# Decode attention over a 4096-key window: keys and values loaded as interleaved pairs of heads in 16 KB rows, the key work of each pair split by rows between VectorE and TensorE

## The chip, the cores and the metric

One core of one Trainium2 chip. The metric is the device time of one execution in microseconds (us). The kernel before took 196.72 us (median of 3 runs, 196.56 to 196.92).

## The reference, cut to what matters

```python
# x: 1 x 1 x 512; k_cache, v_cache: 1 x 32 heads x 32768 x 128, bf16; only the last W = 4096 keys count
q = (layernorm(x) @ wq)                        # 32 heads of 128
scores = q . k_cache[:, :, -4096:] * 128**-0.5 # one query per head
o = softmax(scores) @ v_cache[:, :, -4096:]
s = o.reshape(4096) @ wo                       # wo: 4096 x 512
return x + s * silu(block_B(layernorm(x)))     # B: a small MLP; its first mixing stage sees one position and gives zero
```

Keys and values are 32 heads x 1 MB each, 67.1 MB of the 78.8 MB that the program reads. There is one query per head, so every key and every value is used once.

## The kernel before

```python
G, LAG, K_BUFS, V_BUFS, MOVED = 4, 7, 12, 7, (2, 4)

def load_kv(pool, cache, h):                  # one head, 1 MB: 32 rows of 128 to a partition, 8 KB in one piece
    t = pool.tile([P, NC, Dh], BF16, tag="kv", name="kv")
    load(t[:], cache[0, h, W0:, :].rearrange("(p c) d -> p c d", p=P))
    return t

def k_vector(h, kn):                          # even heads: VectorE multiplies and sums
    ...
    nc.vector.tensor_tensor(out=prod[:], in0=kn[:], in1=q_bc[...].to_broadcast([P, NC, Dh]), op=ALU.mult)
    nc.vector.tensor_reduce(out=st[g]["sS"][:, hl // 2, :], in_=prod[:], axis=AX.X, op=ALU.add)

def k_turn(h, kn):                            # odd heads: TensorE transposes, ScalarE evacuates,
    for b in range(NB):                       # and TensorE multiplies with the query (k_scores)
        pt = ps_tr.tile([P, 8, P], BF16, tag="pt", name="pt")
        for i in range(8):
            nc.tensor.transpose(pt[:, i, :], kn[:, b * 8 + i, :], ident_bf[:])
        nc.scalar.copy(out=kts[h][:, b * 8:(b + 1) * 8, :], in_=pt[:])

for i in range(H + LAG):                      # value head h runs LAG behind key head i
    h = i - LAG
    kn = load_kv(k_pool, A_k_cache, i) if i < H else None
    ...
    v = load_kv(v_pool, A_v_cache, h) if h >= 0 else None
    ...
    if h == H - 1:                            # behind the last values: the output-weight rows of four heads,
        load_rows(H - G, G - 1)               # 512 KB in pieces of 1 KB
        load_rows(H - 1, 1)
    ...                                       # key work, then softmax of a group of four heads, then v_head
for h in range(H - G, H):
    y_head(h)                                 # four row products a head into y_ps
...
nc.vector.tensor_tensor(out=y[:], in0=y_ps[:], in1=g_row[:], op=ALU.mult)     # "the final product"
```

## Time and profile before

| | kernel before |
|---|---|
| time of the profiled execution, span in the profile | 197.07, 195.2 us |
| data moved by the main queue, packets | 78.85 MB, 11344 |
| PE, DVE, ACT busy | 134.2, 124.6, 85.0 us |
| last value head landed, final product began | 189.99, 191.73 us |

The prediction below shows the lines for the busy row, the queue, the chain and the tail. From the timeline of VectorE around the start (columns: start us, us, engine, line, operation, out<-in, count, idle time before and what ended it): the first product with a key.

```profile
25.46 2.29 DVE L278 TENSOR_TENSOR prod<-kv,q_bc 128x4096 bf16<-128x4096 bf16 x1 [1.32 <-ACT q_bc L242]
```

### The profile page before, as it was taken

What the parts mean: (1) busy time and instruction counts of PE and PEld (TensorE: products, weight loads), DVE (VectorE), ACT (ScalarE), POOL (GpSimd) and SP (SyncE); (2) the same over time, 40 slices, a digit from 0 to 9 for tenths busy, and PEclk for the clock granted to TensorE, in tenths of its full rate; (3) what the DMA queues carried; (4) which work ended last, traced back from release to release, by engine and by line L of the source; (5) the groups of instructions that cost most, each with busy time, mean ns of one, the idle gap of its engine ahead of it and who ended that gap; (6) DMA issues with size and microseconds to landing.
All of it is one profiled execution on the core that took longest, in us unless ns stands there. A gap on an engine that the chain in (4) does not pass through costs nothing.

```text
span 195.2 us, 4912 instructions
## 1 busy us (share of the span) xinstructions
PE 134.2 (69%) x2204; PEld 107.8 (55%) x2204; DVE 124.6 (64%) x124; ACT 85.0 (44%) x180; POOL 5.9 (3%) x13
## 2 busy tenths in 40 slices
PE   0559796814994987469988358289788477196952
PEld 0453456803993986464546357174547366195742
DVE  1520279998998988917877674909885678611101
ACT  2003066862954738343366318161638245173010
POOL 2110033000000000000000000000000000000000
PEclk9999998885555555557999855559999555555555
DMA  5999999999999999999999999999999999999980
GB/s 193 408 467 430 384 421 425 413 423 430 421 425 420 423 426 425 421 421 428 430 425 421 421 430 430 423 425 420 428 428 423 425 421 426 423 428 427 421 327 12
DMA packets 11516, 79.15 MB, mean 405 GB/s; under 512 B 1384, under 2 KB 2248, under 8 KB 2504
## 3 DMA queue, kind: packets, MB, share of 16 engines
q1 hardware_dynamic: 11344, 78.85, 96.6%
q8 instruction: 17, 0.28, 0.6%
q10 hardware_dynamic: 152, 0.00, 0.0%
q14 instruction: 3, 0.02, 0.0%
HBM read 78.84 MB, written 0.00 MB: 404 GB/s over the span
## 4 chain that ended last, share of the span: by engine, by line
DMA 81%; PE 12%; issue 3%; DVE 2%; ACT 1%; POOL 1%; SPq 1%; POOLq 0%
DMA kv<-in_A_k_cache_dram 51%; DMA kv<-in_A_v_cache_dram 28%; PE pt L290 2%; DMA x_bf<-in_A_x_dram 2%; PE qb_ps L240 2%; PE hr_ps L214 2%; PE a_ps L203 1%; PE hr_ps L211 1%; PE oT L389 1%; PE qT_ps L231 1%; SPq L77 1%; ACT kt L291 1%; DVE hr L217 0%; PE y_ps L141 0%; PE ln_ps L158 0%
## 5 line engine op out<-in xcount | busy, mean ns | idle before, releaser
L291 ACT COPY kt<-pt 128x1024 bf16<-128x1024 bf16 x64 | 60.1, 1025 | 48.5 <-PE pt L290 48.5
L281 DVE TENSOR_REDUCE sS<-prod 128x32 f32<-128x4096 bf16 x16 | 70.7, 4420 | 0.6
L290 PE MATMUL pt<-ident_bf,kv 128*128 128x128 bf16 x512 | 48.6, 277 | 18.6 <-DMA kv<-in_A_k_cache_dram 17.1
L290 PEld LDWEIGHTS <-kv 128*128 128x128 bf16 x512 | 44.3, 129 | 22.5 <-DMA kv<-in_A_k_cache_dram 19.6
L278 DVE TENSOR_TENSOR prod<-kv,q_bc 128x4096 bf16<-128x4096 bf16 x16 | 36.6, 2286 | 9.6 <-DMA kv<-in_A_k_cache_dram 8.2
L389 PE MATMUL oT<-pT,kv 128*128 128x1 bf16 x768 | 24.1, 165 | 9.4 <-DMA kv<-in_A_v_cache_dram 9.0
L389 PEld LDWEIGHTS <-kv 128*128 128x128 bf16 x768 | 22.9, 104 | 12.3 <-DMA kv<-in_A_v_cache_dram 9.7
L297 PE MATMUL sT<-qT_bf,kt 128*128 128x1 bf16 x512 | 16.4, 164 | 1.9 <-ACT kt L291 1.7
L297 PEld LDWEIGHTS <-kt 128*128 128x128 bf16 x512 | 15.1, 100 | 4.1 <-ACT kt L291 2.3
L379 PE MATMUL ov<-kv,pT 128*4 128x512 bf16 x64 | 15.7, 389 | 1.0 <-DMA kv<-in_A_v_cache_dram 1.0
L404 ACT ACTIVATE o<-oT,rden 128x1 bf16<-128x1 f32 x32 | 6.2, 263 | 16.3 <-PE oT L389 16.3
L336 DVE RECIPROCAL rden<-den_ps 128x4 f32<-128x4 f32 x8 | 1.5, 182 | 16.4 <-PE den_ps L334 16.4
L379 PEld LDWEIGHTS <-pT 128*4 128x4 bf16 x64 | 5.0, 85 | 8.6 <-issue 2.6
L311 PE MATMUL mt_ps<-ident_f,m 128*4 128x128 f32 x8 | 2.9, 359 | 9.1 <-DVE m L305 8.9
L321 PEld LDWEIGHTS mb_ps<-md,ones_f 4*128 4x128 f32 x16 | 3.6, 275 | 6.7 <-DVE md L315 6.5
L321 PE MATMUL mb_ps<-md,ones_f 4*128 4x4 f32 x16 | 4.3, 334 | 4.4 <-DVE md L315 4.4
L313 DVE TENSOR_REDUCE mx<-mt_ps 4x1 f32<-4x128 f32 x8 | 2.2, 278 | 7.7 <-PE mt_ps L311 7.7
L323 ACT COPY mb<-mb_ps 128x4 f32<-128x4 f32 x8 | 1.4, 173 | 12.8 <-PE mb_ps L321 12.8
L311 PEld LDWEIGHTS mt_ps<-ident_f,m 128*4 128x4 f32 x8 | 0.7, 94 | 10.1 <-issue 6.2
L551 DVE TENSOR_TENSOR y<-y_ps,g_row 128x128 f32<-128x128 f32 x1 | 0.3, 291 | 9.2 <-PE y_ps L141 9.2
L217 DVE COPY hr<-hr_ps 1x512 f32<-1x512 f32 x1 | 0.7, 679 | 8.1 <-PE hr_ps L214 8.1
L206 ACT ACTIVATE a_bf<-a_ps 128x10 bf16<-128x10 f32 x1 | 0.2, 180 | 11.5 <-PE a_ps L203 11.5
(110 smaller groups left out, 99.3 us busy)
## 6 DMA issues: line engine op xcount, KB each, us to landing
kv<-in_A_k_cache_dram SPq DMA_DIRECT2D x32, 1024.0 KB, 19.7
kv<-in_A_v_cache_dram SPq DMA_DIRECT2D x32, 1024.0 KB, 19.6
wq_sb<-in_A_wq_dram SPq DMA_DIRECT2D x1, 4096.0 KB, 18.1
wo<-in_A_wo_dram SPq DMA_DIRECT2D x3, 1024.0 KB, 19.6
w_sb<-in_B_w_dram SPq DMA_DIRECT2D x1, 1376.0 KB
w_sb<-in_B_w_dram SPq DMA_DIRECT2D x1, 1024.0 KB
w_sb<-in_B_w_dram SPq DMA_DIRECT2D x1, 512.0 KB, 3.8
wo_rows<-in_A_wo_dram SPq DMA_DIRECT2D x1, 384.0 KB, 15.5
```

The lines of the kernel that those rows point to most:

```text
L214: nc.tensor.matmul(hr_ps[:], lhsT=a_bf[0:m, i:i + 1], rhs=w4_sb[0:m, i, :], start=False, stop=(i == len(chunks) - 1))
L240: nc.tensor.matmul(qb_ps[:], lhsT=xn_rep[:, c, :], rhs=wq_h[:, c, 2 * i:2 * i + 8:2, :], start=(c == 0), stop=(c == KC - 1))
L278: nc.vector.tensor_tensor(out=prod[:], in0=kn[:], in1=q_bc[:, h // 2:h // 2 + 1, :].to_broadcast([P, NC, Dh]), op=ALU.mult)
L281: nc.vector.tensor_reduce(out=st[g]["sS"][:, hl // 2, :], in_=prod[:], axis=AX.X, op=ALU.add)
L290: nc.tensor.transpose(pt[:, i, :], kn[:, b * 8 + i, :], ident_bf[:])
L291: nc.scalar.copy(out=kts[h][:, b * 8:(b + 1) * 8, :], in_=pt[:])
L297: nc.tensor.matmul(st[g]["sT"][:, hl // 2, c:c + 1], lhsT=kt[:, c, :], rhs=qT_bf[:, h:h + 1], start=True, stop=True)
L311: nc.tensor.transpose(mt_ps[:], s["m1"][:], ident_f[:])
L321: nc.tensor.matmul(mb_ps[:], lhsT=ones_f[0:G, :], rhs=s["md"][:], start=True, stop=True)
L379: nc.tensor.matmul(s["ov"][32 * hl:32 * hl + 4], lhsT=s["pT"][:, hl, c:c + 4], rhs=v[:, c:c + 4, :], start=False, stop=c == NC - 4, skip_g ...
L389: nc.tensor.matmul(s["oT"][:, hl:hl + 1], lhsT=v[:, c, :], rhs=s["pT"][:, hl, c:c + 1], start=(c == 0), stop=(c == NC - 1))
L404: nc.scalar.mul(o_blk[h // 8][:, (h + k) % 8:(h + k) % 8 + 1], st[g]["oT"][:, hl + k:hl + k + 1], st[g]["rden"][:, hl + k:hl + k + 1])
```

## The change

The intent: longer rows cost fewer packets. Heads 2i and 2i+1 are loaded as one 2 MB tile whose partitions alternate between the two heads, so that one partition takes 64 consecutive rows of one head, 16 KB. Since a tile now holds two heads, VectorE and TensorE can no longer take a head each; they split the 64 rows. VectorE takes 24 rows in the first four pairs and 40 in the others. The last pair of values comes in two pieces (48 and 16 rows), and the output-weight rows of heads 28 and 29 go between them. The output weights of the first 16 heads come as one block, in rows of 16 KB instead of 8.

```diff
-LAG = 7
-K_BUFS = 12
-V_BUFS = 7
-MOVED = (2, 4)
+LAG = 3
+K_BUFS = 6
+V_BUFS = 3
+EARLY = 4
+MOVED = (1, 3)
+CUT = 48
-    def load_kv(pool, cache, h):
-        t = pool.tile([P, NC, Dh], BF16, tag="kv", name="kv")
-        load(t[:], cache[0, h, W0:, :].rearrange("(p c) d -> p c d", p=P))
+    def load_kv(pool, cache, i, cuts=None):
+        t = pool.tile([P, CP, Dh], BF16, tag="kv", name="kv")
+        src = cache[0, 2 * i:2 * i + 2, W0:, :].rearrange("a (b c) d -> b a (c d)", b=P // 2)
+        dst = t[:].rearrange("p c d -> p (c d)")
+        cuts = cuts or (0, CP)
+        for c0, c1 in zip(cuts, cuts[1:]):
+            load(dst[:, c0 * Dh:c1 * Dh], src[:, :, c0 * Dh:c1 * Dh])
+            if c0 == 0 and c1 < CP:
+                load_rows(H - 4, 2)
         return t
... (query columns for all heads, their rows broadcast by parity; masks for the parity)
+    def nd(s):
+        return 24 if s < EARLY else 40
+    def k_vector(s, kn, half):
+        m = nd(s) // 2
+        rows = slice(m * half, m * half + m)
+        ... multiply and sum these m rows
     def k_turn(s, kn):
+        n = nd(s)
+        ... transpose rows n to 64, eight to a tile
... (products with two columns, one for each head; softmax of two pairs with the other head masked out)
-        if h == H - 1:
-            load_rows(H - G, G - 1)
-            load_rows(H - 1, 1)
+        if last:
+            load_rows(h_part, 2)
+            v = load_kv(v_pool, A_v_cache, h, (0, CUT, CP))
+        elif h >= 0:
+            v = load_kv(v_pool, A_v_cache, h)
+        if last:
+            load_rows(H - 2, 2)
+            ... at the end of the last turn:
+            v_pair(h, v, 0, CUT)
+            for r in range(h_part + 2, H - 2):
+                y_head(r)
+            v_pair(h, v, CUT, CP)
+            v_out(2 * h, 2)
+            for r in range(H - 2, H):
+                y_head(r)
```

## The prediction

> **What bounds the kernel now.** I read the page first: span, engines, slices, queues, chain. Then the synchronisation queue's waits, the transfers of single stretches, the chain of waits in order of time, and the groups by line.
>
> From the page (engine busy times, the 40 slices, the main data queue, the chain by engine and by line):
>
> ```profile
> PE 134.2 (69%) x2204; PEld 107.8 (55%) x2204; DVE 124.6 (64%) x124; ACT 85.0 (44%) x180; POOL 5.9 (3%) x13
> ...
> DMA  5999999999999999999999999999999999999980
> ...
> q1 hardware_dynamic: 11344, 78.85, 96.6%
> ...
> DMA 81%; PE 12%; issue 3%; DVE 2%; ACT 1%; POOL 1%; SPq 1%; POOLq 0%
> ```
>
> No compute engine is over 69%. The DMA row is at nine tenths or more from the second slice to the 38th, and 81% of the chain is transfers. Who held up the issuing of transfers (queue, line, what it waited for, us in total, times, longest):
>
> ```profile
> SPq L77 <- DMA kv<-in_A_k_cache_dram: 64.1, 31, 2.2
> SPq L77 <- DMA kv<-in_A_v_cache_dram: 53.6, 26, 3.3
> ...
> SPq L77 <- PE qb_ps L240: 3.6, 1, 3.6
> ...
> SPq L77 <- PE pt L290: 0.6, 3, 0.3
> ```
>
> The queue waits for older transfers to land, hardly ever for an engine to free a buffer. A 1 MB load lands 19.7 us after its issue (page, DMA issues) and one is issued about every 2.47 us, so eight are always queued. The kernel is a saturated transfer stream with a head and a tail. Only fewer engine-microseconds of transfer, or a shorter tail, can shorten it.
>
> How long is a byte? Two stretches: 12 to 19 us, where only the query weights (32 KB rows) move, and 40 to 180 us, nearly all keys and values (8 KB rows):
>
> ```profile
> DMA packets 91, 2.98 MB, mean 426 GB/s; under 512 B 0, under 2 KB 0, under 8 KB 0
> ...
> q1 hardware_dynamic: 91, 2.98, 98.6%
> ```
>
> ```profile
> DMA packets 8156, 59.46 MB, mean 425 GB/s; under 512 B 910, under 2 KB 910, under 8 KB 910
> ...
> q1 hardware_dynamic: 8141, 59.24, 100.5%
> ```
>
> First: 7 us x 16 engines x 0.986 / 91 = 1213 ns for a 32 KB packet. The trace's packet records, grouped by size (no view prints them), give the same median, 1213 ns, and 309 ns for 8 KB, 159 for 4 KB, 84 for 2 KB, 46 for 1 KB, 9 for the 4-byte completion write. A line through 32 KB and 8 KB: (1213 - 309) / (32768 - 8192) = 0.03678 ns per byte, which is 27.2 GB/s an engine or 435 GB/s for 16, plus 309 - 301.3 = 7.7 ns fixed. Check at 1 KB: 37.7 + 7.7 = 45.4 against 46. So a packet costs 7.7 ns plus its bytes, and a row is one packet.
>
> The tail, from the chain of waits (start us, us, what) and the busy times of 186 to 191 us:
>
> ```profile
> 175.16 14.84 DMA kv<-in_A_v_cache_dram
> ...
> 190.04 1.01 PE oT L389 x32
> 191.05 0.66 PE y_ps L141 x15
> 191.71 0.02 issue
> 191.73 0.30 DVE y L551
> ```
>
> ```profile
> 186.00:191.00 5.00, 3.33 (x104) 2.93 (x104) 0.00 (x0) 0.53 (x2) 0.00 (x0) 0.50 0.74 284
> ```
>
> The last value head lands at 189.99 us and 1.74 us of work follow before the final product. In these last 5 us the DMA engines are busy 0.74: they finish unevenly, and about 5 x 0.26 = 1.3 us is lost.
>
> **What the Trainium skill says.** "DMA: Bandwidth & Descriptors", section "Why small descriptors are slow (HBM only)": each packet pays a fixed few cycles inside the engine. The trace agrees in kind, with 7.7 ns. The same page, "Where 436 GB/s comes from": a ceiling of 435.2 GB/s from the ports; the slope above gives 435. Same page, "Why a DMA increments its semaphore by 16 and not by 1": a load is spread over the largest number of engines up to 16 that divides the slowest dimension of both sides. The new load has 64 x 2 rows on the source and 128 partitions on the destination, so still 16; no run yet shows it. "VectorE: DVE Perf Modes", section "The perf-mode tier table": a reduction has only the 1x mode, a bf16 product the 2x mode. The trace agrees: 4420 ns and 2286 ns for 4096 columns.
>
> **The change, part by part.**
>
> *Transfers, on the path.* Bytes are the same. 64 loads of 1 MB become 32 of 2 MB; the row goes from 8 to 16 KB. A 16 KB packet should take 602.7 + 7.7 = 610 ns. Per engine, 64 x 8 = 512 packets x 309 = 158.2 us become 256 x 610 = 156.2 us: -2.0 us. The last pair is cut into 12 KB and 4 KB rows, eight more packets an engine: +0.06. The first output-weight block gets 16 KB rows: -0.06. About 32 fewer completion writes an engine x 9 ns: -0.3. The packet times overlap by about 1% (share 1.01), so I take not -2.3 but -2.0 us.
>
> *VectorE, beside the stream.* One head in two, 32 of 64 rows of a pair, becomes 24 of 64 in the first four pairs and 40 in the other twelve. One row costs (2286 + 4420) / 32 = 210 ns. So 16 x 32 = 512 rows, 107 us, become 4 x 24 + 12 x 40 = 576 rows, 121 us. A late pair costs 40 x 0.21 = 8.4 us plus half a group's small work (masked merge, maximum, `mx`, `md`, reciprocal, each 0.18 to 0.3, with gaps about 1.6 a group): 9.2 us. The stream brings a pair of keys and a pair of values in 4.19 MB / 429 GB/s = 9.8 us. VectorE keeps pace with 0.5 us to spare: tight.
>
> *TensorE and ScalarE, beside it.* Transposed rows fall from 512 to 4 x 40 + 12 x 24 = 448. Evacuations fall from 64 to 56 x 1025 ns. The score and value products get two columns instead of one, at the same instruction count per row (31 ns each in a train). A late pair costs TensorE 24 x 0.112 (32 transposes took 3.59) = 2.7 us, scores 0.8, values 2.0 (6.1 where moved): under 9.8. An early pair takes ScalarE 5 x 1.03 = 5.1 us.
>
> *Start.* The query columns need 128 products instead of 64 (+1.7 us) and a transpose with two small copies (+0.7); the broadcast falls from 3.5 us to about 1. The first key product moves from 25.5 to about 27.7 us. The first value load waits for that region (27.4 before, 28.5 now), but 8 MB of keys are queued until about 40 us in both versions, so it is hidden.
>
> *Buffers.* Six key and three value buffers of 2 MB are bytes for bytes what twelve and seven of 1 MB were, less one value megabyte. Value load h waits until pair h-3 is consumed. With five 4.9 us loads queued behind that landing, it can be 22 us late. My walk through the order gives VectorE about 8 us behind the keys after the slow start (ScalarE's four times 5.3 us, and the first softmax holding both engines), so a value pair is consumed 6 to 12 us after landing. About 10 us remain, and the output-weight block in the middle gives 4.9 us back.
>
> *Tail.* After the last piece: 16 products (0.5 us) instead of 32 (1.0), two ScalarE scalings (0.45) instead of one (0.26), 8 row products (0.35): 1.5 instead of 1.74 us. But only two heads' rows (0.74 us of 1 KB packets) follow the last values, where four did, so these land later against the end of the stream. I put the net at 0.
>
> Sum: 196.7 - 2.0 = 194.7; with a small chance of a better tail, 194.5 us.
>
> **The rivals.**
> 1. *VectorE becomes the bound.* For it: 9.2 of 9.8 us. If the merge and its waits cost 1 us a pair more, the backlog at the last keys is 8 us instead of about 2. The last keys then come some 24 us before the last values, of which softmax and two value pairs leave some 5 spare, so the end slips 3: 197 to 198 us. Against it: every buffer wait has slack, and the work after the last keys is small.
> 2. *The new row order loads the engines or ports badly.* Two heads lie 8 MB apart, and each engine now alternates between them. "DMA: Bandwidth & Descriptors", "Latency and other measured facts", reports slow transfers at megabyte row pitches. Here the 64 rows of one head stay contiguous, so I expect nothing; if a 16 KB packet took 5% longer, 195 + 8 = 203 us. Nothing in the trace before speaks for it, nor can it exclude it.
> 3. *The tail gains too.* If the uneven finish shrinks by the 1.3 us, or the cut saves more, 193. The 2% mark is 192.8, and even 16 KB packets with no fixed cost at all would save only 512 x 7.7 ns = 3.9 us. So over 2% needs nearly everything.
>
> **Range and chances.** Stream arithmetic is firm to 0.5 us, the tail to 1, rival 1 adds up to 3 on one side: 193.0 to 197.4. Within 2% is 192.8 to 200.7: 0.80. Faster 0.12, slower 0.08, which is rival 2.
>
> **What would show it.** Right: key and value packets of 16 KB at about 610 ns, 429 GB/s in the middle slices, the DMA row still full of nines, VectorE near 141 us. Rival 1: the last values landed well before TensorE takes them, and TensorE waiting for the maximum. Rival 2: 16 KB packets well over 610 ns. Starving: zeros or sevens in the DMA row, with the queue waiting for an engine. I am wrong in mechanism if the time falls by more than 3 us with the packet time as said, or rises with the DMA row still full.

## More of the kernel before

TensorE has nothing to do before each of the last two value heads until it lands; the number in brackets is that idle time.

```profile
187.64 1.10 PE L389 MATMUL oT<-pT,kv 128*128 128x1 bf16 x32 [0.69 <-DMA kv<-in_A_v_cache_dram]
...
190.04 1.01 PE L389 MATMUL oT<-pT,kv 128*128 128x1 bf16 x32 [0.98 <-DMA kv<-in_A_v_cache_dram]
```

## The result, and the profile after

| | before | after |
|---|---|---|
| median of 4 runs of each on one chip | 196.82 us (196.56 to 196.94) | 197.07 us (196.77 to 197.26) |
| time of the profiled execution, span | 197.07, 195.2 | 197.26, 195.4 |
| last value piece landed, final product began | 189.99, 191.73 | 189.30, 191.64 |

The ratio of after to before is 1.0013, with a 95% interval of 0.9996 to 1.0031: the same, where 1.1% less was predicted. Here and below a ratio is the mean time of one kernel's fast runs over that of the other's fast runs of the same rounds, so it is not quite the ratio of the medians.

The page of the kernel after, the four lines that answer to those of before: engines, the DMA row of the 40 slices, the main queue, the chain that ended last.

```profile
PE 142.9 (73%) x2156; PEld 110.4 (56%) x2156; DVE 141.8 (73%) x160; ACT 81.9 (42%) x181; POOL 6.3 (3%) x13
...
DMA  6999999999999999999999999999999999999940
...
q1 hardware_dynamic: 6736, 78.84, 95.4%
...
DVE 47%; PE 28%; ACT 14%; issue 6%; DMA 2%; POOL 1%; ACTq 0%; POOLq 0%
```

VectorE is where it was expected (141.8 us against 141). The DMA row is still full of nines and ends a little earlier: the last slices show 4 and 0 where they showed 8 and 0. But the chain has turned over: 81% transfers have become 2%, and the path now runs through VectorE, TensorE and ScalarE. The stream still runs without gaps while the work beside it has become just as long.

The middle of the run, 40 to 180 us, transfers only:

```profile
DMA packets 4281, 60.00 MB, mean 429 GB/s; under 512 B 477, under 2 KB 541, under 8 KB 541
...
q1 hardware_dynamic: 4268, 59.80, 100.1%
```

59.80 MB against 59.24 MB in the same 140 us, 0.95% more, with half the packets. The packet records give 611 ns for 16 KB (median; 610 predicted). The share fell from 100.5% to 100.1%: the small overlap of the packets went away with the small packets.

The queue that issues the loads, what it waited for (columns: what, us in total, times, longest):

```profile
SPq L77 <- PE den_ps L374: 50.5, 6, 11.4
SPq L77 <- DMA kv<-in_A_v_cache_dram: 26.7, 6, 11.3
SPq L77 <- PE oT L428: 25.4, 4, 13.9
SPq L77 <- PE pt L321: 19.7, 3, 10.0
```

Before, it waited for older transfers and hardly ever for an engine. Now the engines decide when a buffer comes free. The DMA row shows that the stream never starved for it, but the slack is gone.

The tail, from the timeline (L340 is the maximum over the last scores, L428 the value products, L151 the output rows):

```profile
178.87 0.29 DVE L340 TENSOR_REDUCE m<-S 128x2 f32<-128x128 f32 x1
...
182.40 1.87 PE L428 MATMUL oT<-pT,kv 128*128 128x2 bf16 x64
...
186.19 1.87 PE L428 MATMUL oT<-pT,kv 128*128 128x2 bf16 x64
...
188.56 1.42 PE L428 MATMUL oT<-pT,kv 128*128 128x2 bf16 x48 [0.19 <-ACT o L448]
...
189.91 0.38 PE L151 MATMUL y_ps<-wo_rows,o 128*1 128x128 bf16 x8
...
190.22 0.58 PE L428 MATMUL oT<-pT,kv 128*128 128x2 bf16 x16
190.84 0.41 ACT L448 ACTIVATE o<-oT,rden 128x1 bf16<-128x1 f32 x2 [2.33 <-PE oT L428]
191.16 0.43 PE L151 MATMUL y_ps<-wo_rows,o 128*1 128x128 bf16 x8 [0.35 <-ACT o L448]
191.64 0.29 DVE L590 TENSOR_TENSOR y<-y_ps,g_row 128x128 f32<-128x128 f32 x1 [6.11 <-PE y_ps L151]
```

No line of TensorE here waits for a transfer. The last value piece landed at 189.30 us and the 16 products that use it start at 190.22, 0.92 us later, because TensorE is still at the piece before. The busy times of the same 5 us that were shown of before (186 to 191 us: PE, PEld, DVE, ACT, POOL, granted clock, DMA share, GB/s):

```profile
186.00:191.00 5.00, 4.61 (x156) 3.92 (x144) 0.00 (x0) 0.57 (x3) 0.00 (x0) 0.50 0.43 160
```

TensorE is busy 4.61 of 5 us where it was busy 3.33, and the DMA engines 0.43 where they were busy 0.74: now the transfers are done first.

No view prints when each of the 16 DMA engines finished its part of a load; the completion records of the trace do. For the last load of all (output-weight rows, whose completion is the end of the stream):

```
             first engine   middle   last engine
before          187.42      190.69      191.35
after           185.90      189.08      189.94      1.52, 1.60 and 1.41 us earlier
```

So the stream itself did get shorter by about 1.5 us, and the time did not. Account at the end of the profiled executions:

- the last engine finishes 1.41 us earlier (predicted 2.0);
- the last values land only 189.99 - 189.30 = 0.69 us earlier, because the rows of two heads now come ahead of them: 0.72 given back;
- from that landing to the final product it takes 191.64 - 189.30 = 2.34 us instead of 191.73 - 189.99 = 1.74: 0.60 given back.

So the final product starts 0.09 us earlier. A fourth term lies behind it: from its start to the end of the span it takes 195.40 - 191.64 = 3.76 us instead of 195.20 - 191.73 = 3.47, 0.29 given back. The work on data is the same there. In the records, two of SyncE's closing semaphore checks start 0.49 us apart (193.99 and 194.48) where the kernel before has 0.07; why is not known. The sum is -1.41 + 0.72 + 0.60 + 0.29 = +0.20 us, and the two profiled times differ by 197.26 - 197.07 = +0.19.

This is one profile of each kernel. The second profile of after (experiment 5) has the order and the closing again, but not the 0.60.

### The profile page after: what moved, and what is told of

Its sections match the earlier page's. It is cut to its first block, busy times and chain, and to the rows that moved or that the text cites. A ratio compares the mean times of both kernels' runs of the same rounds, so it can differ in the third digit from the quotient of the medians.

```text
span 195.4 us, 4829 instructions
## 1 busy us (share of the span) xinstructions
PE 142.9 (73%) x2156; PEld 110.4 (56%) x2156; DVE 141.8 (73%) x160; ACT 81.9 (42%) x181; POOL 6.3 (3%) x13
## 4 chain that ended last, share of the span: by engine, by line
DVE 47%; PE 28%; ACT 14%; issue 6%; DMA 2%; POOL 1%; ACTq 0%; POOLq 0%
DVE S L310 26%; DVE prod L308 15%; ACT kt L322 11%; PE ov L417 6%; PE oT L428 4%; PE yr_ps L489 3%; PE hr_ps L222 2%; PE pt L321 2%; DMA x_bf<-in_A_x_dram 2%; PE qT_ps L238 2%; PE y_ps L151 2%; PE a_ps L211 1%; DVE m L340 1%; PE qb_ps L250 1%; PE mb_ps L359 1%
## 5 line engine op out<-in xcount | busy, mean ns | idle before, releaser
L310 DVE TENSOR_REDUCE S<-prod 128x20 f32<-128x2560 bf16 (+1 forms) x32 | 81.7, 2553 | 1.1
L322 ACT COPY kt<-pt 128x1024 bf16<-128x1024 bf16 x56 | 52.8, 1024 | 24.9 <-PE pt L321 24.9
L308 DVE TENSOR_TENSOR prod<-kv,q_bc 128x2560 bf16<-128x2560 bf16 (+1 forms) x32 | 43.2, 1349 | 2.7 <-ACT q_bc L252 2.4
L321 PE MATMUL pt<-ident_bf,kv 128*128 128x128 bf16 x448 | 41.8, 275 | 1.3 <-DMA kv<-in_A_k_cache_dram 0.8
L321 PEld LDWEIGHTS <-kv 128*128 128x128 bf16 x448 | 39.4, 130 | 4.6 <-issue 3.6
L327 PE MATMUL sT<-qT_bf,kt 128*128 128x2 bf16 x448 | 18.7, 166 | 13.6 <-ACT kt L322 12.9
L417 PE MATMUL ov<-kv,pT 128*8 128x512 bf16 x64 | 22.3, 525 | 0.0
L428 PE MATMUL oT<-pT,kv 128*128 128x2 bf16 x768 | 22.1, 165 | 0.2 <-ACT o L448 0.2
L428 PEld LDWEIGHTS <-kv 128*128 128x128 bf16 x768 | 21.3, 102 | 1.3 <-issue 1.2
L417 PEld LDWEIGHTS <-pT 128*8 128x8 bf16 x64 | 6.7, 110 | 14.4 <-issue 12.1
L368 ACT ACTIVATE pT<-S,mb 128x64 bf16<-128x64 f32 x32 | 10.9, 356 | 0.2
```

What stands on the lines that cost most here:

```text
L308: nc.vector.tensor_tensor(out=prod[:, 0:m, :], in0=kn[:, rows, :], in1=q_bc[:, s:s + 1, :].to_broadcast([P, m, Dh]), op=ALU.mult)
L310: nc.vector.tensor_reduce(out=st[s // 2]["S"][:, s % 2, rows], in_=prod[:, 0:m, :], axis=AX.X, op=ALU.add)
L321: nc.tensor.transpose(pt[:, i, :], kn[:, n + b + i, :], ident_bf[:])
L322: nc.scalar.copy(out=kts[s][:, b:b + 8, :], in_=pt[:])
L327: nc.tensor.matmul(st[s // 2]["sT"][:, s % 2, c, :], lhsT=kt[:, c, :], rhs=qT_bf[:, 2 * s:2 * s + 2], start=True, stop=True)
L368: nc.scalar.activation(out=s["pT"][:, i // 2, :, i % 2], in_=s["S"][:, i // 2, :], func=ACT.Exp, scale=scale, bias=mb[:, i:i + 1], accum_o ...
```

## The experiments

The theory after the result: two things in the tail gave the gain back, the order of the last rows, and a TensorE that is late because VectorE's last keys are late. The rivals: the stream gained less than the packets say; or the tail is held by something that neither explains. They went to the chip in four calls; in each, all kernels were timed beside the kernel before on the same chip (11 runs of it in each call; medians 196.82, 196.81, 196.93 and 197.01).

### 1. VectorE relieved: 32 rows instead of 40

```diff
-        return 24 if s < EARLY else 40
+        return 24 if s < EARLY else 32
```

> Only VectorE's share of a late pair falls from 40 to 32 rows (12 x 8 = 96 rows x 0.21 us = 20 us less VectorE work, TensorE and ScalarE get 96 more rows). Theory A (the end is set by a compute backlog: VectorE finishes the last keys at 178.9 us and TensorE then reaches the last value piece 0.95 us after it landed at 189.27): VectorE finishes the last keys before 175 us, TensorE waits for the last value transfer, and the time falls by 0.6 to 0.9 us to about 196.3. Theory B (the end is set by the end of the transfer stream and its uneven finish; the compute chain only ends near it): no change, 197.0 within 0.2.

197.07 us (196.88 to 197.97), ratio 1.0012 to the kernel before, with its 95% interval [0.9986, 1.0039]: no gain. (All ratios below are to the kernel before.) The timeline of the tail:

```profile
188.17 1.44 PE L428 MATMUL oT<-pT,kv 128*128 128x2 bf16 x48 [2.14 <-DMA kv<-in_A_v_cache_dram]
...
190.03 0.58 PE L428 MATMUL oT<-pT,kv 128*128 128x2 bf16 x16
...
191.45 0.29 DVE L590 TENSOR_TENSOR y<-y_ps,g_row 128x128 f32<-128x128 f32 x1 [8.99 <-PE y_ps L151]
```

The cause that it was to remove is removed: the last maximum ends at 176.1 us instead of 179.2, TensorE waits 2.14 us for the values, and the work after the last landing is 191.45 - 189.98 = 1.47 us. But this landing moved from 189.30 to 189.98. The first engine finished that piece at 185.13 (185.23 in after) and the middle one at 188.41 (188.43); only the last engine was 0.68 us later. The instruction queue carried 18 packets instead of 17 (384 more TensorE instructions), which made instruction packets a suspect. The edit's gain was cancelled by something that it did not aim at, so this run alone does not price the late TensorE.

### 2. The rows of heads 28 and 29 behind the last values

```diff
-            if c0 == 0 and c1 < CP:
-                load_rows(H - 4, 2)
 ...
-            load_rows(H - 2, 2)
+            load_rows(H - 4, 4)
 ...   (and their row products behind the products of the last value piece)
```

> Only the order of the last transfers: the rows of heads 28 and 29 (256 KB in 1 KB packets, about 0.75 us of stream) go behind the last value piece, and their products behind its products. VectorE's share stays 40. Theory A: the last piece lands about 0.7 us sooner, but TensorE isn't there yet, so the time stays within 0.3 us of the changed kernel (about 197). Theory B: the end follows the landing, 0.5 to 0.7 us faster (about 196.4).

196.41 us (195.90 to 197.10), ratio 0.9973 [0.9946, 1.0000]. TensorE now takes the last values at 187.47 us, and it waits for transfers again, 0.43 us for the values and 0.46 for the rows:

```profile
187.47 2.03 PE L426 MATMUL oT<-pT,kv 128*128 128x2 bf16 x64 [0.43 <-DMA kv<-in_A_v_cache_dram]
...
189.96 0.59 PE L149 MATMUL y_ps<-wo_rows,o 128*1 128x128 bf16 x16 [0.46 <-DMA wo_rows<-in_A_wo_dram]
190.61 0.29 DVE L588 TENSOR_TENSOR y<-y_ps,g_row 128x128 f32<-128x128 f32 x1 [6.41 <-PE y_ps L149]
```

The final product began 1.03 us earlier than in after. It looked like the repair. It was run again:

> The kernel with the rows behind (e2) once more, as yardstick for the next three and to see whether its 0.27% under the kernel before repeats: 196.4 us within 0.4.

197.02 us (196.41 to 197.83), ratio 1.0007 [0.9980, 1.0035]. The profile was as good (the final product began at 190.58), the times were not; the profiled execution itself took 196.75 us with the span of 194.2 us that 196.03 us had, so about 0.7 us of it lie outside the span. Its twelve runs have a mean of 196.8 us against 196.9 of the kernel before. The gain did not repeat, and no faster version is claimed.

### 3. Both at once

> Both edits. Theory A: with TensorE on time the earlier landing counts too: 1.2 to 1.5 us under the changed kernel, about 195.7, which is about 1.1 us under the kernel before. Theory B: as with the order alone, about 196.4.

196.75 us (196.51 to 197.69), ratio 0.9996 [0.9970, 1.0023]. TensorE waits 1.96 us for the values and 0.63 us for the rows, so no engine holds the end any more; but the rows landed at 190.39 instead of 189.92, again with 18 instruction packets. The transfers hold the end, at a time that is no better. The profile says where the rest went: the last load ends 191.35 - 190.39 = 0.96 us earlier than in the kernel before, but all 16 row products now follow it, so that the final product comes 0.69 us behind it instead of 0.38, and the closing takes 3.65 us instead of 3.47.

### 4. The length of the rows alone

The kernel of experiment 1 with each pair loaded as two transfers of 8 KB rows:

```diff
-        cuts = cuts or (0, CP)
+        cuts = cuts or (0, CP // 2, CP)
 ...   (the last pair of values keeps its two pieces)
```

> The kernel with 32 late rows, and each 2 MB pair loaded as two transfers of 8 KB rows (same bytes, same buffers, same compute). This prices the 16 KB rows alone where the stream sets the end. By the prediction's sum 2.0 us; by the two streams' ends (191.04 against 189.61 us) 1.4 us. So: theory A says 1.2 to 2.0 us slower than the kernel with 32 late rows (about 197.9), packets of 8 KB at 309 ns and 425 GB/s. If row length were worth nothing in the time, as the bare result suggests, it equals the kernel with 32 late rows.

198.54 us (197.71 to 199.13), ratio 1.0070 [1.0035, 1.0104], 1.47 us over experiment 1. In the stretch from 60 to 180 us its main queue moved 50.74 MB where that of experiment 1 moved 51.18, 0.86% less: the price of the short rows, near the 0.95% between after and before. But the six times fall into two groups, 197.71 to 197.99 and 199.08 to 199.13, and the profiled run (199.13) is of the second. Its query weights, which this edit does not touch, came slowly; transfers from 12 to 19 us, of this kernel and then of after:

```profile
DMA packets 85, 2.79 MB, mean 398 GB/s; under 512 B 0, under 2 KB 0, under 8 KB 0
...
q1 hardware_dynamic: 85, 2.79, 103.2%
```

```profile
DMA packets 93, 3.05 MB, mean 435 GB/s; under 512 B 0, under 2 KB 0, under 8 KB 0
...
q1 hardware_dynamic: 93, 3.05, 100.7%
```

7 x 16 x 1.032 / 85 = 1.36 us for a 32 KB packet against 7 x 16 x 1.007 / 93 = 1.21. So an execution can lose about 1 us on its first weights. This was seen in three of the 16 profiles (here, in experiment 7 and in 12), none of them of the kernel before; that it makes the whole upper group of times is not shown. Without that group the row length is worth 197.8 - 197.1 = 0.7 us in the times, with it 1.5. In its profile the closing takes only 3.12 us, against 3.74 in experiment 1; if it does so in the other runs, the 0.7 is 1.3 at the final product. The length of the rows did what it was to do; its exact size is not settled.

### 5. The kernel after again

> The changed kernel itself, beside the next three on one chip, as their yardstick: 197.0 us within 0.3, the ratio to the kernel before 1.00.

197.06 us (196.94 to 198.50), ratio 1.0026 [1.0002, 1.0050]. The result stands: no gain. Its profile (197.04 us, span 194.97) is a second one of the kernel after:

```profile
189.79 0.58 PE L428 MATMUL oT<-pT,kv 128*128 128x2 bf16 x16
...
191.21 0.29 DVE L590 TENSOR_TENSOR y<-y_ps,g_row 128x128 f32<-128x128 f32 x1 [6.15 <-PE y_ps L151]
```

The last value piece landed at 189.49 us and the last load ended at 190.13. Against the profile of the kernel before, the stream is 1.22 us earlier, the order gives back 0.72 again and the closing 0.29 again. But the work after the landing is 191.21 - 189.49 = 1.72 us, no more than the 1.74 before: TensorE starts 0.30 us late, not 0.92. A last 0.2 us lie outside the span: time less span is 2.04 to 2.10 us in five of these six runs, 1.73 to 1.91 in 44 runs of the kernel before. Of the four terms of the first account, then, the late TensorE is the one that did not repeat.

### 6. The kernel before with the new order of the last rows

```diff
+        if h == H - 1:
+            load_rows(H - G, 2)
         v = load_kv(v_pool, A_v_cache, h) if h >= 0 else None
 ...
-            load_rows(H - G, G - 1)
-            load_rows(H - 1, 1)
+            load_rows(H - 2, 2)
```

> The kernel BEFORE with the order of the last transfers that the change introduced: the output rows of heads 28 and 29 go ahead of the last value head, only 30 and 31 behind it. If the change gave back part of its stream gain by that order (256 KB of 1 KB packets, 16 x 46 ns = 0.74 us per engine, moved ahead of the last values), this alone costs the kernel before 0.6 to 0.8 us: about 197.5. If the order is worth nothing, the time stays at 196.8.

197.35 us (197.25 to 197.63, five fast runs), ratio 1.0029 [1.0017, 1.0041], that is 0.54 us slower by the medians. In its timeline the wait for the last value head grows from 0.98 to 1.68 us and the end with it:

```profile
190.63 1.01 PE L389 MATMUL oT<-pT,kv 128*128 128x1 bf16 x32 [1.68 <-DMA kv<-in_A_v_cache_dram]
...
192.32 0.29 DVE L552 TENSOR_TENSOR y<-y_ps,g_row 128x128 f32<-128x128 f32 x1 [9.90 <-PE y_ps L141]
```

Where the transfers alone set the end, the order of the rows costs 0.54 us. This is the cleanest price: one part of the change on the old kernel, with an interval that excludes no effect.

### 7. More TensorE instructions

510 tiny products of zeros, on the kernel of experiment 2, to test the instruction packets:

```diff
+            if s in (4, 7, 8, 11, 12, 14):
+                for _ in range(85):
+                    nc.tensor.matmul(y_ps[:, 0:2], lhsT=zero_bf[:], rhs=ident_bf[:, 0:2], start=False,
+                                     stop=False, skip_group_check=True)
```

> The kernel with the rows behind (e2) and 510 extra one-pass products of zeros on TensorE (1020 instructions, 15 us of TensorE time, spread over six pairs where it has slack; result unchanged). Theory: TensorE's instructions are fetched through the same DMA engines in 16 KB packets, one per 256 instructions, each delaying one engine by 0.6 to 1.1 us, and the slowest engine sets when a load has landed. Then the instruction queue shows 21 packets instead of 17, the first and the middle engine land the last rows as before (185.7 and 188.8 us), the last engine 0.5 to 1.5 us later, and the time rises by as much. Rival: what made the 32-row kernels no faster is TensorE's or ScalarE's longer work; then the landings stay and only waits for TensorE grow, or nothing changes at all.

204.34 us, ratio 1.0396 [1.0367, 1.0425]. This test failed in its purpose. The padding was not free for the work beside the stream: the last maximum moved from 177.8 to 186.8 us, and the last value products wait for ScalarE, not for data:

```profile
186.48 0.28 DVE L338 TENSOR_REDUCE m<-S 128x2 f32<-128x128 f32 x1
...
196.18 1.84 PE L426 MATMUL oT<-pT,kv 128*128 128x2 bf16 x64 [0.19 <-ACT o L446]
```

It says nothing of instruction packets. It does say that the changed kernel's engine work has little slack: 12 us more of busy TensorE (154.5 against 142.4) made it 7.5 us slower than the kernel before.

### 8. VectorE relieved at the start instead

The kernel of experiment 2 with 32 rows for VectorE in the first four pairs (an edit of the 24 in `nd`).

> The kernel with the rows behind (e2), and VectorE taking 32 instead of 24 rows of the first four pairs: 32 rows fewer on TensorE and ScalarE, 128 TensorE instructions fewer (half an instruction packet). VectorE gets 6.7 us more work where it waited for the others. Theory: the stream decides, so 0 to 0.4 us under e2 (196.0 to 196.4). Rival: VectorE's chain decides, and the added work makes it slower than e2 by 1 us or more.

197.55 us (195.81 to 198.96, one of them slow), ratio 1.0015 [0.9971, 1.0058]. Three runs lie at 195.8 to 196.7 and three at 198.4 to 199.0. Nothing can be read from it but the scatter.

### 9. Instruction packets from an engine that nobody waits for

GpSimd writes one word 1024 times, on the kernel of experiment 2. Nothing waits for it and no other engine uses the word.

```diff
+        if s == LAG:
+            idle = small.tile([P, 1], FP32, name="idle")
+            for _ in range(1024):
+                nc.gpsimd.memset(idle[:], 0.0)
```

> e2 with 1024 tiny clears on the idle GpSimd (four more 16 KB instruction packets, no work for the other engines). Theory of instruction packets: the instruction queue shows 21 or so packets, the middle engine lands the last rows as in e2 (188.8 us), the slowest one 0.3 to 1.5 us later, and the time rises by about that. If instruction packets don't matter: time and landings as in e2.

201.49 us (201.47 to 201.77), ratio 1.0232 [1.0208, 1.0256]: 4.6 us slower than the kernel before, for instructions beside everything. The page's lines for the two queues of instructions, then the tail:

```profile
q8 instruction: 17, 0.28, 0.6%
q14 instruction: 11, 0.09, 0.1%
```

```profile
192.95 1.89 PE L426 MATMUL oT<-pT,kv 128*128 128x2 bf16 x64 [2.23 <-DMA kv<-in_A_v_cache_dram]
...
195.68 0.60 PE L149 MATMUL y_ps<-wo_rows,o 128*1 128x128 bf16 x16 [0.85 <-DMA wo_rows<-in_A_wo_dram]
```

Queue 14 carries 11 packets of 8 KB instead of 4, spaced about 20 us over the whole run (the records: 60.0, 80.3, 100.5, 120.4, 140.0, 160.3 us among them). The last load:

```
                      first engine   middle   last engine
rows behind (exp. 2)     185.68      188.83      189.92
with GpSimd's writes     187.39      190.62      195.64
```

Middle and first engine finish about 1.7 to 1.8 us later, the last one 5.7: the difference between first and last grows from 4.2 to 8.3 us. Near five of these packets (80.3 to 160.3 us) it grows by 0.64 to 0.92 us each, near the one at 60.0 by 0.16. The largest step, 2.5 us between the landings at 163.92 and 171.33, is not theirs: two loads of output weights (`wo_few`, 128 KB each, in both kernels) have only four completions, which makes 8 packets of 309 ns on each of four engines, and the slowest engine is one of the four. In after, too, four engines fall back there by 2.4 us.

That an instruction packet holds the engine that carries it is seen directly in the packet records of after: of 4050 data packets of 16 KB behind the first 22 us, 16 take more than 640 ns. Each of the 16 begins as an instruction packet ends (within 0.03 us) and takes 1.08 to 1.27 us instead of 0.61; the instruction packets before them take 1.0 to 1.17 us (16 KB) or 0.31 to 0.33 (8 KB). So it is shown that a load is complete when the slowest of the engines is, and that instruction packets, which travel through the same engines, hold one engine back by more than their own time. The size was larger than any theory had it. The 1.7 us that all engines lost are not explained. Nor was it tested apart whether GpSimd's 1024 writes, and not only their instructions, cost something.

### 10. The reciprocal moved out of VectorE's way

VectorE waits 10.0 us in all for the sums of the softmax (`den_ps`) ahead of its reciprocals; the edit does each reciprocal half a pair later (`nc.vector.reciprocal` moved from `sm_den` into a step of its own), once on the kernel of experiment 2 and once on after.

> e2 with VectorE's reciprocal of the softmax sums put after its next half pair of keys, so that it no longer waits for TensorE's value products there (10.0 us of waits in the changed kernel). Same instructions, only the order. If the compute backlog is part of what ate the gain: VectorE ends the last keys before 176 us instead of 178, TensorE waits for the last values by over 1 us, and the time falls 0.2 to 0.6 us under e2 and scatters less. If the stream alone decides: as e2.

> The same reciprocal move on the changed kernel itself, with its order of the last rows. Backlog theory: TensorE is on time for the last values, the work after their landing falls from 2.3 to 1.5 us, and the time falls by 0.5 to 0.8 us to about 196.4. If the order of the last rows alone ate the gain: no change, 197.0.

196.25 us (196.03 to 197.64), ratio 0.9975 [0.9947, 1.0003], and 197.15 us (196.52 to 199.33), ratio 1.0026 [0.9987, 1.0065]. The last maximum ended at 179.05 and 178.94 us, against 179.16 in after: the move did not bring VectorE forward, so neither run tests what a shorter backlog is worth. The first has the best median together with experiment 2, but its interval too includes no effect.

### 11 and 12. VectorE relieved in the last four pairs only

Experiment 1 had 384 more instructions. Here only the last four pairs go to 32 rows, 128 more instructions and no further packet; 12 is the kernel after with that edit alone, 11 has the rows of experiment 2 as well.

```diff
-        return 24 if s < EARLY else 40
+        return 24 if s < EARLY else 32 if s >= 12 else 40
```

> The kernel after with VectorE taking 32 rows instead of 40 in the last four pairs only, and nothing else. Tie theory: last maximum at 174 to 176 (179.16 in after), TensorE waits 1 to 2 us for the last value pieces, work after the last landing 1.5 us instead of 2.34, with the landing where after had it (189.3 to 189.5): 196.2 to 196.5, that is 0.5 to 0.9 us below after. Rival, the backlog is not what made TensorE late: no change of the work after landing, 197.0 to 197.2. Rival, instruction packets: landing 0.3 to 0.7 us later, 196.8 to 197.1.

> The kernel after with the rows of heads 28 and 29 behind the last values, as in e2, and VectorE taking 32 rows instead of 40 in the last four pairs only (8 x 4 rows, 6.7 us less at the end, 128 more TensorE instructions, half an instruction packet). Tie theory (the work of the last keys and the landing of the last values end within a microsecond of each other, so both must be relieved): last maximum 3 to 5 us earlier than in e2 (177.8), TensorE waits for the last value piece and for the last rows, 195.9 to 196.3, 0.5 to 0.9 us below the kernel before and 0.3 to 0.6 below e2. Rival, the order of rows alone: as e2, 196.4 to 197.0. Rival, instruction packets: landings 0.3 us later than e2 and no gain.

12, the relief alone: 196.58 us (196.11 to 198.02), ratio 0.9980 [0.9956, 1.0004] to the kernel before; after stood at 1.0013 in the first comparison and 1.0026 in experiment 5, so by these ratios the relief is worth 0.33% to 0.46%, or 0.6 to 0.9 us (with the scatter of both). The account above has 2.34 - 1.5 = 0.8 for it, the profile of experiment 5 only 1.72 - 1.5 = 0.2. Its backlog went as intended: the last maximum begins at 176.04 us, although this profile is of an execution with slow first weights (198.02 us, the slowest of the six; 87 packets of 32 KB from 12 to 19 us), and TensorE waits 2.07 us for the values, later 0.88 us for the rows, so the work after the last values cannot be read from it:

```profile
176.04 0.29 DVE L340 TENSOR_REDUCE m<-S 128x2 f32<-128x128 f32 x1
...
188.72 1.44 PE L428 MATMUL oT<-pT,kv 128*128 128x2 bf16 x48 [2.07 <-DMA kv<-in_A_v_cache_dram]
```

11, both: 197.00 us (196.18 to 197.70), ratio 1.0002 [0.9977, 1.0026]. It was to be the best of all, 195.9 to 196.3, and that fell. In its timeline nothing but transfers holds the end: TensorE waits 2.11 us for the values and 1.27 for the rows.

```profile
187.53 1.86 PE L426 MATMUL oT<-pT,kv 128*128 128x2 bf16 x64 [2.11 <-DMA kv<-in_A_v_cache_dram]
...
190.66 0.60 PE L149 MATMUL y_ps<-wo_rows,o 128*1 128x128 bf16 x16 [1.27 <-DMA wo_rows<-in_A_wo_dram]
191.31 0.29 DVE L588 TENSOR_TENSOR y<-y_ps,g_row 128x128 f32<-128x128 f32 x1 [9.91 <-PE y_ps L149]
```

Its last load: first engine 185.90, middle 189.05, last 190.62 us. First and middle engine are those of after (185.90, 189.08); the last is 0.68 us later, with 17 instruction packets as in after. So the number of these packets alone does not settle where the slowest engine ends: profiles with the same bytes and the same 17 packets end at 189.47, 189.92, 189.94 and 190.62 us.

## Why the prediction was wrong

**Right:** the kernel before is a transfer stream; a 16 KB packet takes 611 ns (610 predicted); the middle slices run at 429 GB/s; VectorE is busy 141.8 us (141) and its last two pairs take 18.7 us (169.49 - 160.50, then to 179.16), 9.3 each, against 9.2; the DMA row stays full; and the last values come 189.30 - 165.71 = 23.6 us after the last keys, "some 24". The result lies inside the range and in the likeliest class, at the far side of the forecast.

**The stream, -2.0 us: a term of the right kind and too large.** At the first, the middle and the last engine of the last load it is 1.4 to 1.6 us earlier (1.2 to 1.5 in experiment 5's profile). The discount for overlapping packets was 0.3 us; the share fell from 100.5% to 100.1%, 0.4% of 140 us, so about 0.6 us of overlap went away with the short packets. 2.3 - 0.6 = 1.7 is near what was measured; the small rest is not accounted for.

**The tail, "I put the net at 0": this step failed.** It comes out at +1.6 us in the first profile (0.72 in the order of the rows, 0.60 in the work after the landing, 0.29 behind the final product) and at +1.0 in the second (0.72, 0 and 0.29), where another 0.2 lie outside the span.
- The order was seen ("these land later against the end of the stream") and not counted, though the numbers were there: 0.74 us of rows moved ahead. On the kernel before it costs 0.54 us (experiment 6).
- The work after the last piece was priced at 1.5 us, as if TensorE stood waiting. It does so in experiment 1 (1.47 us). In after TensorE is late and it takes 2.34 us in one profile and 1.72 in the other.
- What follows the final product was not looked at. It takes 3.76 us in both profiles of after against 3.47 in the kernel before and 3.45 in experiment 6.

**Why TensorE is late: the walk through the backlog, which said "about 2" us at the last keys and "some 5 spare".** The last keys landed at 165.71 us, VectorE's own work on them takes 9.67 us (169.49 to 179.16), so it was 179.16 - 165.71 - 9.67 = 3.8 us behind. From the last maximum to the final product TensorE and ScalarE need 191.64 - 179.16 = 12.5 us with no wait for data. To begin the final product 1.5 us after the last landing, at 190.8, the maximum must end at 178.3; without any backlog it would end at 165.71 + 9.67 = 175.4. The spare was 2.9 us, not 5, and the backlog 3.8, not 2. In experiment 5's profile the maximum ends at 178.69 and the last piece lands at 189.49, which leaves TensorE only some 0.2 us behind: it is a near tie, and small shifts decide it. Part of it comes from the start, where the first key product was put at 27.7 us:

```profile
23.75 3.50 PE qT_ps L238 x128
```

```profile
30.41 0.96 DVE L308 TENSOR_TENSOR prod<-kv,q_bc 128x1536 bf16<-128x1536 bf16 x1 [2.36 <-ACT q_bc L252]
```

The first line is from the chain of waits of after, the second from its timeline. 1.6 us of the shift from 25.46 to 30.41 were there before the query products began (`hr` is copied at 22.06 instead of 20.50). That part need not be the change's: in experiment 6 the old kernel has 21.65 and 27.48. From `hr` to the first product it is 4.96 us in before, 5.83 in experiment 6, and 8.35 in after, so the change itself moved the start by some 2.5 to 3.4 us, where 2.2 were predicted.

**The rivals.** The first, VectorE as the bound, was the nearest: the chain is VectorE's and TensorE's now. But its number (197 to 198 us by three microseconds of slip) had another make-up; the slip is 0.8 us in one profile and 0.2 in the other, and the time comes from the row order and the closing too. The second fell: no packet is slower for the alternation of heads. The third fell: the uneven finish is as large as before, 3.9 us between first and last engine in the kernel before and 4.0 in after. The prediction's own test, "wrong in mechanism if the time ... rises with the DMA row still full", is met as far as the row goes; the time did not fall, and its rise of 0.1 to 0.3% is hardly more than the noise.

**Shown, argued, open.** Shown: the stream became shorter by 1.2 to 1.6 us (two profiles); the order of the rows costs 0.54 us where transfers set the end; relieving VectorE makes TensorE wait for data again; a load ends with its slowest engine, and instruction packets hold engines back. Argued from profiles and not shown by times: that the terms add up in after; the closing was undone by no experiment. Undone singly, they bring it to between 0.5 us below the kernel before and 0.2 above (experiments 1, 2 and 12), with intervals that include no difference; undone together (experiments 3 and 11), to no difference at all. Then only transfers hold the end. The slowest engine ended between 189.5 and 190.6 us from one profile to the next, against 191.35 in before, and the row products behind it and the closing took about 0.5 us more than before (experiment 3). Open: what decides on which engine the instruction packets and the `wo_few` loads meet (the records have no engine's number), what makes the closing longer, and why some executions get their first weights 1 us late; together these are as large as the gain that was looked for.

## What to carry to other kernels

When a stream is made shorter, ask what ends together with it: here the engines' work finished within two microseconds of the transfers, and a gain of 1.5 us in the stream ran into it and into the order behind it. Follow the account to the last instruction: it closed only with the 0.29 us behind the final product, and a term that one profile shows (0.60) can be absent from the next. Count every transfer that is moved ahead of the last needed one at its full length, and check a balance of engines at the last tile by the whole path from there (landing, backlog, own work, the work behind it), not by the average of a tile. A load is finished when its slowest DMA engine is; a mean rate of 429 GB/s says nothing of that engine, and the end of one profile says little of the next.

## What the Trainium skill lacked or had wrong

- "Runtime: NRT & Kernel Launch", section "Instruction fetch mechanics", says that instructions come in 16 KiB blocks of 256 and that crossing a block is mostly hidden. The blocks of TensorE agree: its 4312 instructions in after made 17 packets of 16 KB; GpSimd's packets had 8 KB. That it is hidden holds for the fetching engine at best: the packets pass through the engines that carry the data, the 16 KB data packet behind one took 1.08 to 1.27 us instead of 0.61, and with seven more of 8 KB (GpSimd's) the kernel was 4.6 us slower than the kernel before (experiment 9). No page read here says what a fetch costs the data stream.
- "DMA: Bandwidth & Descriptors", section "Why a DMA increments its semaphore by 16 and not by 1": the load of alternating heads was spread over 16 engines, as the page's rule has it (16 completions). What the page lacks is how far apart they finish: 4.0 us in after for a load of 256 KB at the end of a full stream, growing over the run.
- No page has by how much the packets of a full stream overlap: those of 8 KB by about 0.5% of the time (share 100.5% in the middle of the run), those of 16 KB by 0.1%. In the first pair of profiles 1.4 to 1.6 us were gained of the 2.3 that the sum of the packets gives.
- No page has that an execution can get its first 32 KB packets slowly, 1.36 us each instead of 1.21 in experiment 4, which put the end of these weights about 1 us later (three of 16 profiles).
